# A gated mix of a long convolution and a mixer MLP: the transforms' second steps as 32x32 products

## The chip, the cores and the metric

The kernel runs on one core of one Trainium2 chip. The metric is the device time of one execution in microseconds (us); before the change the median of three runs is 244.84 us (244.6 to 245.31).

## The reference, cut to what matters

Shapes: S = 2048 tokens, D = 640 channels, F = 1536; everything is bf16.

```python
g = sigmoid((x * gate_w).sum(-1, keepdims=True))          # x is A_q
# A: a short convolution of k over 4 tokens, times v, then a long causal convolution
k_shift = sum over t of k_pad[:, t:t+S, :] * shift_k[:, 3-t]
kv = k_shift * v
y  = irfft(rfft(kv padded to 2S) * rfft(ssm_k padded to 2S))[:S] + kv * ssm_D
a  = x * y
# B: a shift mixer and an MLP
h  = gelu(layernorm(x) @ w1)
hs = concat(the four quarters of h, shifted by +1, -1, +2, -2 tokens) @ w2
x1 = x + hs
b  = x1 + gelu(layernorm(x1) @ w3) @ w4
out = g * a + (1 - g) * b
```

## The kernel before, in words

Tokens lie as 128 partitions x 16 rows ("u"), so a row of 128 tokens x 640 channels is one tile. The work is some 1,000 small tasks (`add(...)`), and `ORDER` lists for each engine, by task number, the order in which it does them. `Plan.schedule` replays these lists with prices written beside each task, and uses the result only to hand out buffers and to emit the instructions. All PSUM tiles come from one tag, `pm`, of four buffers, each of two banks: a buffer holds 128 x 640 as two halves of 320 (`HD`).

Branch B: `norm`, `first_product` (w1), `second_product` (w2), `norm` again, `third_product` (w3, called for four groups of four rows) and `fourth_product` (w4, three tasks of eight matmuls for each row). For twelve rows an addition of the row (line 941) follows on VectorE and then a scaling by 1-g (`scaled`); the last four rows (`early`: 14, 15, 0, 1) are finished by one fused instruction (line 998).

Branch A: the long convolution is a discrete transform of length 4096 in two steps. `step1` multiplies with 128 x 128 sine tables `F1` (line 803), for the filter (H) and for kv (X), and stores into the DRAM tiles `SH` and `SX`. The second step is 32 small transforms. `forward` (line 869) loads 16 frequencies with all channels (`read_b`, lines 858 to 862) and does two matmuls of 128 x 128 x 320 for each of 32 values of t, for H and for X; the stationary matrices `M2`, `G1`, `G2` are block-diagonal, 3/4 zeros, and are made from sines by copies under masks (lines 424 to 428 and 499 to 502). Each pair of filter results is copied to SBUF scaled (line 888), and two DMAs exchange its lower and upper 64 partitions into a second copy (lines 891 and 892, 32 DMAs in all). The X result is copied to SBUF, one product on VectorE (line 906) multiplies it with the filter and with its exchanged copy, and four matmuls (line 914) go back; the result is copied and stored into `SZ`. At the end `SZ` is loaded, transformed by `F1T` (line 972), scaled by the gate, multiplied with x and added.

The first `RUNS` tasks on TensorE are matmuls of the identity (line 360) that compute nothing which is used; a list can put them anywhere.

Of the kernel before, what the change touches and what calls it, by code (L numbers as in the profile page):

```python
# [10 lines left out]
ALU = mybir.AluOpType  # L11
# [8 lines left out]
        48 49 40 41 43 42 51 77 81 80 117 121 53 59 65 83 171 165 177 175 173 135 90 131 357 361 368 363 372  # L20
        370 366 359 364 185 179 149 189 145 191 187 375 381 377 193 390 388 203 386 384 205 163 272 399 397
        395 393 273 406 402 408 274 404 199 201 275 413 415 417 411 418 285 213 422 426 420 424 207 215 288
        432 436 217 434 430 219 286 801 445 61 287 439 443 446 450 807 448 816 56 454 57 452 459 813 457 804
        461 463 66 504 300 313 301 470 810 472 298 466 479 481 477 475 314 312 512 510 490 311 499 491 493
        497 299 839 845 518 842 851 848 854 619 629 624 617 622 634 639 524 526 532 534 632 627 642 637 649
        538 654 540 659 546 548 797 652 821 664 552 662 657 674 877 679 560 562 883 684 934 689 568 880 576
        886 699 692 677 704 582 709 892 707 719 712 724 588 729 697 717 596 889 722 739 744 604 602 737 610
        608 742 752 747 764 869 769 757 762 767 780 874 924 946 918 921 915 930 959 927 973 912 942 975 967
        969 982 989 984 1000 998 1007 1005 897
    """,  # L30
    "DVE": """
        96 34 47 13 37 107 39 44 108 109 110 111 52 115 114 78 45 118 119 64 122 123 58 84 72 124 125 126
        136 137 129 138 132 133 139 140 128 86 87 89 91 146 142 147 324 143 325 150 151 152 153 154 326 327
        328 156 379 329 160 330 161 157 222 331 159 225 332 228 333 231 334 335 234 336 283 277 237 279 62
        281 243 337 60 338 240 339 68 340 341 441 342 267 343 55 264 344 54 345 346 261 294 255 347 252 67
        348 349 350 258 249 296 246 468 351 352 290 506 353 354 830 292 355 835 782 484 488 825 486 495 793
        783 795 791 520 792 69 305 790 303 820 796 307 320 787 794 785 781 789 614 786 309 615 63 620 863
        625 788 630 640 784 635 858 644 650 645 873 318 660 655 798 554 868 316 647 831 665 669 670 322 667
        675 680 672 566 685 690 687 694 574 682 695 700 705 580 710 702 714 590 715 720 730 594 725 734 732
        735 727 740 749 750 826 901 745 754 759 755 760 765 896 770 772 911 864 906 952 954 902 938 955 961  # L40
        962 859 907 836 956 963 976 977 970 971 1015 991 1017 992 993 985 1001 1008 1002 1009 986 1011 1013
    """,
    "PE": """
        23 32 33 16 18 50 31 28 29 22 26 76 21 30 79 27 17 116 25 120 24 82 172 164 170 176 174 85 134 88
        130 356 367 360 20 362 369 371 365 358 188 184 178 148 190 144 186 19 374 376 378 380 192 389 387
        202 385 383 220 221 204 162 158 223 224 398 394 396 392 226 227 229 405 401 230 407 198 403 200 232
        233 414 412 235 416 410 236 212 241 242 421 425 214 419 423 206 238 239 431 435 216 433 429 218 800
        799 440 444 265 266 438 805 262 263 442 806 449 815 253 254 814 447 259 260 811 453 812 451 250 458
        251 802 456 803 460 462 256 257 503 247 248 808 244 245 469 467 809 471 465 827 828 505 478 829 480
        476 832 474 833 511 509 834 822 823 487 483 824 489 817 496 485 498 818 492 494 819 837 838 519 844  # L50
        843 840 841 517 850 849 846 847 852 853 613 618 860 861 623 628 862 616 621 633 855 638 525 523 856
        533 531 857 631 626 643 641 636 648 870 539 537 653 871 658 872 545 651 865 547 866 553 867 663 646
        661 551 876 656 668 673 875 678 666 882 559 671 561 881 683 565 879 567 688 878 686 885 693 573 575
        884 681 698 691 676 703 890 581 579 708 891 701 706 713 718 711 589 723 696 587 728 887 716 593 595
        888 733 731 721 738 726 743 898 603 748 601 899 609 736 900 607 751 741 753 893 758 763 746 894 768
        756 895 761 766 908 771 909 903 910 904 913 905 914 922 923 916 920 917 919 928 929 958 960 951 925
        953 926 939 972 943 966 974 940 941 968 981 944 990 988 945 983 999 997 1004 1006 931 932 935 933
        936 937
    """,
    "POOL": """  # L60
        15 14 46 35 36 71 73 112 113 74 127 93 94 92 95 167 141 182 155 168 166 169 180 183 195 38 194 197
        181 196 276 208 210 211 75 289 209 302 315
    """,
    "SP": """
        0 6 1 7 2 8 3 4 9 10 97 99 98 5 70 373 11 12 100 382 101 391 400 102 409 103 284 278 282 280 427 104
        437 501 515 105 428 455 106 464 297 268 271 473 295 482 291 269 293 270 500 529 502 513 514 508 507
        521 516 306 308 530 304 522 543 310 527 528 536 535 773 557 544 541 542 549 558 550 571 556 555 774
        572 317 323 563 564 586 569 570 775 578 585 577 776 583 584 321 599 591 592 777 598 319 597 600 778
        606 605 611 612 779 947 949 950 948 964 965 979 980 995 996 978 957 1018 994 1016 1003 1010 1012 987
        1014  # L70
# [109 lines left out]
def kernel(  # L180
# [22 lines left out]

    nc = tc.nc
# [35 lines left out]
    XPR = WS[0][:].rearrange("p (s a d) -> p s a d", s=4, d=D)  # L240
    HTA = WS[1][:].rearrange("p (n d) -> p n d", d=D)
    W4 = WS[1][:].rearrange("p (k d) -> p k d", d=D)
    GEN = [WS[2][:, 2048 * t:2048 * t + 2048].bitcast(I32) for t in range(3)]
# [4 lines left out]
    M2 = const("M2", [P, KH, 2, 4, 16], BF16)  # L248
    G1 = const("G1", [P, KH, 4, 2, 16], BF16)
    G2 = const("G2", [P, KH, 4, 2, 16], BF16)  # L250
# [15 lines left out]
    SH = dram.tile([32, P, D], BF16, name="SH")  # L266
    SX = dram.tile([32, P, D], BF16, name="SX")
    SZ = dram.tile([4, 32, 32, D], BF16, name="SZ")

    sizes = {"g": S, "xnt": DT * 512, "r": D, "u4": 4 * P, "xp": 0}  # L270
    counts = {"g": 3, "xnt": 2, "r": 6, "u4": 2, "xp": 4, "pm": 4}
# [53 lines left out]
    LW1 = dma("SP", 800, lambda: W1N, lambda: B_w1.rearrange("(kt p) n -> p kt n", p=P))  # L325
    QL += [load_q(2), load_q(3)]
    HNB, LH = [], []
    for dt in range(DT):
# [5 lines left out]
        tensor=B_w2.tensor, offset=B_w2[0, 0].offset, ap=[[D, P], [CG * D, 4], [1, D]])),  # L334
           dma("SP", 160, lambda: W2P[:, 4, :], lambda: bass.AP(
               tensor=B_w2.tensor, offset=B_w2[P, 0].offset, ap=[[CG * D, 4], [D, R], [1, D]]))]
# [41 lines left out]
    names = ["basep", "basei", "offp0", "offi0", "offp1", "offi1", "midp", "kli", "klf"]  # L378
    cmask = [3, 15, 4, 64, 4, 64, 120, 48, 3]
    cmul = [16.0, 512.0, -512.0, -64.0, -512.0, -64.0, 0.125, 0.0625, 1.0]  # L380
    cadd = [1.0, 1.0, 6144.0, 6144.0, 8192.0, 4096.0, 0.0, 0.0, 0.0]
# [4 lines left out]
    mk = const("mk", [P, 2, 4])  # L386
    val = {n: cv[:, i:i + 1] for i, n in enumerate(names)}

    def do_rows(e):
        for dst, vals in ((cm[:, 0, :], cmask), (ca[:, 0, :], cmul), (ca[:, 1, :], cadd)):  # L390
            i = 0
            while i < NC:
                j = i
                while j < NC and vals[j] == vals[i]:
# [5 lines left out]
    icf, ick, icn, m1 = (GEN[0][:, 0:512], GEN[0][:, 512:1024], GEN[1][:, 0:512],  # L400
                         GEN[1][:, 512:1024].bitcast(F32))

    def do_iota(e):
        nc.gpsimd.iota(icf.rearrange("p (g i n) -> p g i n", i=4, n=16), pattern=[[64, 8], [4, 4], [512, 16]],
                       base=0, channel_multiplier=0)
        nc.gpsimd.iota(ick.rearrange("p (g i n) -> p g i n", i=4, n=16), pattern=[[64, 8], [4, 4], [0, 16]],
                       base=0, channel_multiplier=0)
        nc.gpsimd.iota(icn.rearrange("p (m n) -> p m n", n=16), pattern=[[0, KH], [1, 16]],
                       base=0, channel_multiplier=0)
# [3 lines left out]
    def do_consts(e):  # L413
# [4 lines left out]
        nc.vector.scalar_tensor_tensor(out=val["basei"], in0=val["kli"], scalar=16.0, in1=val["basei"],  # L418
                                       op0=ALU.mult, op1=ALU.add)
# [4 lines left out]
    def do_masks(e):  # L424
        for n, kl in enumerate((val["klf"], val["kli"])):
            for j in range(4):
                nc.gpsimd.tensor_scalar(out=mk[:, n, j:j + 1], in0=kl, scalar1=float(j), scalar2=None,
                                        op0=ALU.is_equal)

    t_consts = add({"DVE": 1.0}, do_consts, [t_rows, t_pidx])  # L430
    t_masks = add({"POOL": 1.3}, do_masks, [t_consts])
# [17 lines left out]
    for o in range(2):  # L449
        ph[0].append(add({"ACT": 0.73, "DVE": 0.45}, lambda e, o=o: affine(  # L450
            e, GEN[0][:, 512 * o:512 * o + 512], m1, 1.0, val[f"offi{o}"]), [t_m1] + ph[2]))
    p0 = add({"DVE": 0.45}, lambda e: nc.vector.tensor_scalar(
        out=GEN[1][:, 0:512], in0=m1, scalar1=0.0, scalar2=None, op0=ALU.add), [t_m1])
    ph[1].append(add({"DVE": 0.45}, lambda e: nc.vector.tensor_scalar(
        out=GEN[1][:, 512:1024], in0=m1, scalar1=6144.0, scalar2=None, op0=ALU.add), ph[0] + [p0]))

    def step1_phase():
        g = genf()
# [434 lines left out]
    for t in range(KH):  # L893
        kg = t // 4
        if t % 4 == 0:
            zg = buf("ct")
# [139 lines left out]
```

## Time and profile before

| | |
|---|---|
| median of three runs | 244.84 us |
| the profiled execution | 245.43 us |
| its span of instructions | 243.6 us |
| granted TensorE clock in it | 0.997 |
| matmuls | 1,513, busy 230.6 us |
| VectorE (DVE) busy | 195.4 us |
| ScalarE (ACT) busy | 170.0 us |
| GpSimd (POOL) busy | 46.8 us |
| moved by DMA | 62.21 MB, mean 255 GB/s |

The span runs from the first to the last instruction of the program; 1.8 us of the profiled time lie around it. Busy time of TensorE counts each matmul up to its modelled end, so that matmuls overlap; where a step from one start to the next is given below, it is the difference of two starts, or of merged lengths. Weight loads (PEld) are listed by themselves.

### The profile page before, as it was taken

What the parts mean: (1) busy time and instruction counts of PE and PEld (TensorE: products, weight loads), DVE (VectorE), ACT (ScalarE), POOL (GpSimd) and SP (SyncE); (2) the same over time, 40 slices, a digit from 0 to 9 for tenths busy, and PEclk for the clock granted to TensorE, in tenths of its full rate; (3) what the DMA queues carried; (4) which work ended last, traced back from release to release, by engine and by line L of the source; (5) the groups of instructions that cost most, each with busy time, mean ns of one, the idle gap of its engine ahead of it and who ended that gap; (6) DMA issues with size and microseconds to landing.
All of it is one profiled execution on the core that took longest, in us unless ns stands there. A gap on an engine that the chain in (4) does not pass through costs nothing.

```text
span 243.6 us, 4200 instructions
## 1 busy us (share of the span) xinstructions
PE 230.6 (95%) x1513; PEld 144.1 (59%) x1530; DVE 195.4 (80%) x334; ACT 170.0 (70%) x256; POOL 46.8 (19%) x103
## 2 busy tenths in 40 slices
PE   7999698879999999999999999999999899999992
PEld 3666454556555556677545777655667576456771
DVE  7999999969899979997897857887887753029892
ACT  6599886879879498884554787687996740467450
POOL 8508129933271500000420000000000000000000
PEclk9999999999999999999999999999999999999998
DMA  5999869809889997689899399999999827990244
GB/s 198 401 397 280 339 163 349 275 27 309 260 222 288 341 350 263 174 302 281 278 265 275 97 235 340 264 335 269 357 261 263 271 78 243 344 377 8 108 155 172
DMA packets 38263, 62.21 MB, mean 255 GB/s; under 512 B 12739, under 2 KB 28355, under 8 KB 38242
## 3 DMA queue, kind: packets, MB, share of 16 engines
q1 hardware_dynamic: 35378, 57.84, 76.0%
q10 hardware_dynamic: 2640, 3.28, 3.8%
q0 software_dynamic: 224, 0.82, 0.9%
q8 instruction: 12, 0.20, 0.4%
q14 instruction: 9, 0.07, 0.1%
HBM read 35.71 MB, written 18.35 MB: 222 GB/s over the span
## 4 chain that ended last, share of the span: by engine, by line
PE 71%; ACT 9%; POOL 6%; DVE 5%; DMA 5%; issue 2%; SPq 0%; DVEq 0%; POOLq 0%; ACTq 0%
PE pm L697 19%; PE pm L682 18%; PE pm L660 7%; PE pm L803 5%; DMA vt<-vt 5%; PE pm L623 4%; PE pm L869 4%; PE pm L914 4%; POOL GS L643 4%; PE pm L972 4%; PE pm L360 3%; DVE W L906 2%; ACT ar L298 2%; ACT W L298 1%; PE pm L723 1%
## 5 line engine op out<-in xcount | busy, mean ns | idle before, releaser
L697 PE MATMUL pm<-W,g 128*128 128x320 bf16 x384 | 57.9, 299 | 0.0
L682 PE MATMUL pm<-xnt,W 128*128 128x512 bf16 x228 | 54.9, 379 | 0.5
L697 PEld LDWEIGHTS <-g 128*128 128x128 bf16 x384 | 37.6, 98 | 14.9
L298 ACT CAST ar<-pm 128x640 bf16<-128x640 f32 x57 | 37.1, 709 | 11.4 <-PE pm L803 9.6
L612 ACT ACTIVATE g<-pm 128x1024 bf16<-128x1024 f32 x24 | 24.5, 1026 | 20.2 <-PE pm L682 19.9
L682 PEld LDWEIGHTS <-W 128*128 128x128 bf16 x240 | 23.5, 98 | 23.7
L906 DVE TENSOR_TENSOR W<-W,vt 128x1280 bf16<-128x1280 bf16 x32 | 25.7, 820 | 6.6 <-DMA vt<-vt 4.9
L660 PE MATMUL pm<-W,GS 128*128 128x320 bf16 x160 | 24.9, 299 | 1.4 <-POOL GS L643 1.2
L767 DVE TENSOR_TENSOR ct<-kt,kt 128x640 bf16<-128x640 bf16 (+3 forms) x25 | 22.7, 944 | 0.0
L914 PE MATMUL pm<-W,G 128*128 128x320 bf16 x128 | 21.1, 299 | 0.6 <-DVE W L906 0.6
L300 ACT ACTIVATE vt<-pm 128x640 bf16<-128x640 f32 x24 | 16.5, 705 | 7.4 <-PE pm L869 6.5
L660 PEld LDWEIGHTS <-GS 128*128 128x128 bf16 x160 | 15.4, 98 | 8.9 <-POOL GS L643 1.8
L643 POOL COPY GS<-u 32x512 bf16<-32x512 bf16 (+4 forms) x20 | 16.9, 854 | 16.3 <-ACT u L612 15.7
L623 PE MATMUL pm<-xnt,W 128*128 128x512 bf16 x76 | 19.2, 379 | 0.8 <-ACT xnt L298 0.4
L803 PEld LDWEIGHTS <-F 128*128 128x128 bf16 x128 | 12.5, 98 | 11.6 <-issue 4.7
L298 ACT CAST ct<-pm 128x640 bf16<-128x640 f32 x23 | 15.4, 697 | 5.3 <-PE pm L914 5.0
L767 DVE TENSOR_TENSOR ct<-ct,ct 128x2560 bf16<-128x2560 bf16 x12 | 18.2, 1518 | 0.2
L298 ACT CAST W<-pm 128x640 bf16<-128x640 f32 x23 | 15.9, 698 | 2.5 <-PE pm L869 2.5
L665 DVE SCALAR_TENSOR_TENSOR Q<-pm,Q 128x640 bf16<-128x640 f32 x16 | 13.1, 821 | 4.4 <-PE pm L660 2.8
L869 PEld LDWEIGHTS <-M 128*128 128x128 bf16 x128 | 12.5, 98 | 6.7 <-issue 0.2
L551 DVE TENSOR_SCALAR r<-Q,mv,rs 128x640 bf16<-128x640 bf16 x32 | 15.5, 505 | 1.0 <-POOL rs L538 0.9
L914 PEld LDWEIGHTS <-G 128*128 128x128 bf16 x128 | 12.4, 98 | 6.6 <-DVE W L906 1.0
(106 smaller groups left out, 339.5 us busy)
## 6 DMA issues: line engine op xcount, KB each, us to landing
cc<-SH SPq DMA_DIRECT2D x8, 640.0 KB, 5.8
kt<-SX SPq DMA_DIRECT2D x8, 640.0 KB, 5.5
vt<-vt SPq DMA_DIRECT2D x32, 160.0 KB, 4.8
SZ<-ct SPq DMA_DIRECT2D x7, 640.0 KB, 5.8
W<-in_B_w_dram SPq DMA_DIRECT2D x2, 1920.0 KB, 12.7
SH<-ar SPq DMA_DIRECT2D x6, 640.0 KB, 4.2
SX<-ar SPq DMA_DIRECT2D x6, 640.0 KB, 3.9
g<-in_A_ssm_k_dram SPq DMA_DIRECT2D x5, 512.0 KB, 10.4
```

The costliest lines, as they stand in the source:

```text
L298: nc.scalar.copy(out=o, in_=i)
L612: nc.scalar.activation(out=o, in_=i, func=ACT.Gelu_apprx_tanh)
L623: nc.tensor.matmul(ps.tile[:, j, :], lhsT=w, rhs=xv()[:, dt, :], start=(dt == 0), stop=(dt == DT - 1))
L643: lambda o, i: nc.gpsimd.tensor_copy(out=o, in_=i)), [t, t_edges], [u4])
L660: nc.tensor.matmul(ps.tile[:, h, 0:HD], lhsT=GS[:, nt, u, :], rhs=W2P[:, nt, h * HD:(h + 1) * HD], start=(nt == 0), stop=(nt == DT - 1))
L682: nc.tensor.matmul(ps.tile[:, j, :], lhsT=W3[:, dt, (f + j) * P:(f + j + 1) * P], rhs=xv()[:, dt, :], start=(dt == 0), stop=(dt == DT - 1))
L697: nc.tensor.matmul(ps.tile[:, h, 0:HD], lhsT=gv[:, ft % 4, i * P:(i + 1) * P], rhs=W4[:, ft, h * HD:(h + 1) * HD], start=(ft == 0), stop=( ...
L767: nc.vector.tensor_tensor(out=o, in0=a, in1=b, op=op)
L803: nc.tensor.matmul(ps.tile[:, comp, 0:HD], lhsT=F1[:, comp, :], rhs=src()[:, 2 * hf + n, h * HD:(h + 1) * HD], start=True, stop=True)
L869: nc.tensor.matmul(ps.tile[:, h, 0:HD], lhsT=M2[:, t].rearrange("p a b c -> p (a b c)"), rhs=tokens(b.tile[:])[:, t % 4, h * HD:(h + 1) * ...
L906: prods = [add({"DVE": 0.75}, lambda e, t=t, xp=xp, hv=hv: nc.vector.tensor_tensor(out=XPR[:, xp.slot, 1:3, :], in0=XPR[:, xp.slot, 0:1, : ...
L914: nc.tensor.matmul(ps.tile[:, h, 0:HD], lhsT=gm[:, t].rearrange("p a b c -> p (a b c)"), rhs=XPR[:, xp.slot, 1 + a, h * HD:(h + 1) * HD], ...
```

## The change

1. **Second step.** `forward` now takes a group of 16 frequencies (kg) and one half h of the channels and does sixteen matmuls of 32 x 32 x 320, one for each pair of row quadrant kl and column quadrant i, into two `pm` buffers. The way back does thirty-two such matmuls into two buffers, two sums of sixteen. `M2`, `G1`, `G2` lose their zeros; masks and masked copies go.
2. **Exchanged filter rows.** The 32 exchanging DMAs go. A second stationary matrix `M2S`, with sine and cosine columns exchanged, gives the exchanged rows by a second `forward` for H, which is copied out of PSUM as well.
3. **Residual.** `fourth_product` begins with two matmuls of the identity with the row, so that the addition on VectorE goes; the scaling by 1-g now reads PSUM. Fused endings remain for rows 0 and 1 only; their `fourth_product` comes after the product with x, which goes into `XQ`.
4. **Layouts.** `SH`, `SX` and `SZ` are partition-major; the products' operands have eight slots, four of them in a new tile `XP2`, which also holds the phases (`GEN`); so the load of w3 no longer waits for the sines. The filter matrix for `F1T` is transposed without a copy before it.
5. **Order.** `ORDER` is new for all engines (955 tasks).

```diff
-    counts = {"g": 3, "xnt": 2, "r": 6, "u4": 2, "xp": 4, "pm": 4}
+    counts = {"g": 3, "xnt": 2, "r": 6, "u4": 2, "xp": 8, "pm": 4}
...
-    LW3 = dma("SP", 1920, lambda: W3, ..., [SIN[2], SIN[3], SIN[4]])
+    MB.append(add({"DVE": 0.6, "ACT": 1.2}, do_m2s, [MB[0]]))
+    LW3 = dma("SP", 1920, lambda: W3, ...)
...
-            prev = add({"PE": 1.09}, mm, done[f0 // 2:f0 // 2 + 2] + [w4, prev], [ps, G[f0 // 4]])
+                for h in range(2 if f0 == 0 else 0):
+                    nc.tensor.matmul(ps.tile[:, h, 0:HD], lhsT=IDB[:], rhs=qrow(u)[:, h * HD:(h + 1) * HD],
+                                     start=True, stop=False)
...
+            prev = add({"PE": 1.09 if f0 else 1.36}, mm, done + [w4, prev] + after, [ps, G[f0 // 4]])
...
-                tensor=dst.tensor, offset=dst[r0, 0, 0].offset, ap=[[D, P], [P * D, 4], [1, D]]),
+                tensor=dst.tensor, offset=dst[0, r0, 0].offset, ap=[[32 * D, P], [1, 4 * D]]),
...
-            ap=[[P * D, 32], [4 * D, 4], [1, 4 * D]]), after, [b])
+            ap=[[D, P], [P * D, 4], [1, D]]), after, [b])
...
+    def quad(i):
+        return slice(32 * i, 32 * i + 32)
+
+    def forward(kg, h, mat, b, ld, dests, after):
+        ps = [buf("pm"), buf("pm")]
         def mm(e):
-            for h in range(2):
-                nc.tensor.matmul(ps.tile[:, h, 0:HD], lhsT=M2[:, t].rearrange("p a b c -> p (a b c)"),
-                                 rhs=tokens(b.tile[:])[:, t % 4, h * HD:(h + 1) * HD], start=True, stop=True)
-        return ps, add({"PE": 0.272}, mm, [ld] + MB[0], [b, ps, dest])
+            for kl in range(4):
+                for i in range(4):
+                    nc.tensor.matmul(ps[kl // 2].tile[quad(i), kl % 2, 0:HD],
+                                     lhsT=mat[quad(kl), 4 * kg + i].rearrange("p a b -> p (a b)"),
+                                     rhs=tokens(b.tile[:])[quad(kl), i, h * HD:(h + 1) * HD],
+                                     start=True, stop=True)
+        return ps, add({"PE": 0.26}, mm, [ld, MB[0] if mat is M2 else MB[3]] + after, [b] + ps + dests)
...
-            HS[t // 2] = [dma("SP", 80, lambda a=a, hv=hv: hv()[64 * (1 - a):64 * (2 - a), 1, :, :],
-                              lambda a=a, hv=hv: hv()[64 * a:64 * (a + 1), 0, :, :], HS[t // 2], [hb]) for a in range(2)]
+            for a, mat in ((0, M2), (1, M2S)):
+                ps, last_h[kg] = forward(kg, h, mat, *BH[kg], [hb], [])
+                for q in range(2):
+                    HS[kg, h].append(add({"ACT": 0.61, "DVE": 0.75}, lambda e, a=a, q=q, ps=ps, hv=hv: copy(
+                        e, hv()[:, a, 2 * q:2 * q + 2, :], half(ps[q]), 1.0 / S), [last_h[kg]], [ps[q], hb]))
...
+                for a, gm in ((0, G1), (1, G2)):
+                    for i in range(4):
+                        for kl in range(4):
+                            k = kl % 2
+                            nc.tensor.matmul(ps[i // 2].tile[quad(kl), i % 2, 0:HD],
+                                             lhsT=gm[quad(i), 4 * kg + kl].rearrange("p a b -> p (a b)"),
+                                             rhs=XPR[xp[kl // 2].slot][quad(i), 1 + a, k * HD:(k + 1) * HD],
+                                             start=(a == 0), stop=(a == 1))
+            z = add({"PE": 0.47}, mm, prods + MB[1:3], xp + ps + [zg])
...
-    early = set(US[3])
+    early = set(US[3][2:])
...
-            if k < 3:
-                t = add({"DVE": 0.76}, lambda e, u=u, ps=ps: nc.vector.tensor_tensor(
-                    out=halves(qrow(u)), in0=half(ps), in1=halves(qrow(u)), op=ALU.add), [t4] + Y[k][3], [ps])
...
-            scaled[u] = add({"ACT": 0.7, "DVE": 0.28}, lambda e, u=u: copy(
-                e, qrow(u), qrow(u), OMG[:, u:u + 1]), [t, t_gate] + Y[k][3])
+                scaled[u] = add({"ACT": 0.65, "DVE": 0.85}, lambda e, u=u, ps=ps: copy(
+                    e, halves(qrow(u)), half(ps), OMG[:, u:u + 1]), [t4, t_gate] + Y[k][3], [ps])
```

Of the new lists, what the prediction uses, by the tasks' contents:

- SP, at the start: the second and first half of q's rows 0 to 3, filter parts 0 and 1, rows 4 to 7 of q, filter parts 2, 3, 4, q's last group, w1, q's third group. Before, w1 and the third group of q came ahead of filter parts 3 and 4.
- POOL, at the start: the small constants and three iotas now come ahead of the identity matrix.
- PE: ahead of the first matmul of `third_product`'s second group, two of the `RUNS` fewer than before, three forward rounds (before: four times two matmuls) and the residual of four rows. From there to the last matmul of the way back: 24 tasks of `third_product`, 24 of `fourth_product`, 45 forward rounds, 16 returns, 2 of the `RUNS`. After it: 12 of `third_product`, 16 last transforms, 12 of `fourth_product`. In two places rounds follow one another with nothing large between: nine tasks (seven forward, two back) and, with one of the `RUNS` in it, eight (six and two).
- Evictions and products of the second step: VectorE had 26 of the 96 evictions and now has 53 of 128; ScalarE had 70 and now has 75. The 32 products stay with VectorE.

## The prediction

> **What bounds the kernel now.** I read the page's busy shares, then the stretches between landmarks, then the timeline of TensorE.
>
> ```profile
> PE 230.6 (95%) x1513; PEld 144.1 (59%) x1530; DVE 195.4 (80%) x334; ACT 170.0 (70%) x256; POOL 46.8 (19%) x103
> ...
> PE   7999698879999999999999999999999899999992
> ```
>
> PE is nearly always busy, but matmuls overlap in that count, so what matters is the step from start to start. Two neighbours in the timeline, and the groups of transposes:
>
> ```profile
> 140.56 1.25 PE L697 MATMUL pm<-W,g 128*128 128x320 bf16 x8
> 141.65 1.25 PE L914 MATMUL pm<-W,G 128*128 128x320 bf16 x8
> ...
> L869 PE MATMUL pm<-kt,M 128*128 128x320 bf16 x64 | 13.1, 299 | 0.1
> ...
> 22.46 0.72 PE L579 MATMUL pm<-IDB,r 128*128 128x128 bf16 x10 [0.28 <-ACT u L612]
> ```
>
> Eight products of 320 columns take 141.65 - 140.56 = 1.09 us, 0.136 each, though one lasts 0.299. Five of 512 columns take 1.08. The transposes step by (0.72 - 0.22)/9 = 0.056: the quickest weight load and matmul seen here.
>
> With 1.079 for a task of `third_product`, 1.087 for one of `fourth_product`, 0.272 per pair of products, 0.543 for four and 0.432 for a warm-up, I sum TensorE's work in three stages. Stage 1 goes to the first matmul of `third_product`'s second group (117.8), stage 2 to the last on the way back (199.05), stage 3 to the end.
>
> ```profile
> 0.00:50.00 50.00, 43.01 (x310) 25.37 (x313) 46.63 (x105) 39.82 (x56) 28.90 (x83) 1.00 0.84 293
> 50.00:117.80 67.80, 67.13 (x431) 42.69 (x438) 61.09 (x90) 53.69 (x92) 13.86 (x16) 1.00 0.82 259
> 117.80:199.00 81.20, 80.24 (x516) 50.71 (x520) 64.55 (x108) 57.96 (x86) 3.99 (x5) 1.00 0.94 264
> 199.00:243.60 44.60, 40.22 (x260) 25.36 (x260) 23.16 (x33) 18.54 (x23) 0.00 (x0) 0.98 0.52 192
> ```
>
> (Columns: stretch, length, busy PE, PEld, DVE, ACT, POOL, clock, DMA share, GB/s.) Stage 1: 105.3 of work in 117.8, the hole being the start (DVE is busy 46.6 of the first 50 us). Stage 2: 80.25 in 81.2. Stage 3: 40.1 in 40.3, then 4.2 of last eviction and store. From 50 us on the array is full: there the time is TensorE's work.
>
> **The change part by part.**
>
> *Second step.* Before: 128 forward products and 128 back, 256 x 0.136 = 34.8 us. After: 1,280 pairs of a weight load and a product of 32x32x320. No row shows such a pair. Low end: sixteen at once, a round at the step of one product, 0.136, a return at 0.272: 48 x 0.136 + 16 x 0.272 = 10.9 us. High end: no overlap, 1,280 x 0.136 = 174 us; the quickest pair seen gives 1,280 x 0.056 = 71.7. I take the prices in the diff, 0.26 and 0.47 (16 ns a pair): 48 x 0.26 + 16 x 0.47 = 20.0 us. They are the planner's, not measured here; but its other prices meet their rows (0.272 for 0.272, 1.08 for 1.079, 0.57 for ten transposes, 0.545 for 0.543), and 0.26 and 0.47 are no simple share of those. This is the weakest step.
>
> *Evictions.* 96 become 128.
>
> ```profile
> L302 DVE CAST W<-pm 128x640 bf16<-128x640 f32 x9 | 7.4, 823 | 4.3 <-PE pm L869 4.2
> ...
> L298 ACT CAST W<-pm 128x640 bf16<-128x640 f32 x23 | 15.9, 698 | 2.5 <-PE pm L869 2.5
> ...
> L906 DVE TENSOR_TENSOR W<-W,vt 128x1280 bf16<-128x1280 bf16 x32 | 25.7, 820 | 6.6 <-DMA vt<-vt 4.9
> ...
> L941 DVE TENSOR_TENSOR Q<-pm,Q 128x640 bf16<-128x640 f32 x12 | 9.9, 822 | 7.0 <-PE pm L697 7.0
> ```
>
> Back to back DVE steps by 0.735, ACT by 0.59. DVE: 27 more evictions +19.8, twelve additions gone -8.9, scalings from PSUM +3.6, masks and small copies -6.0, others -5.4: about +3 over the kernel. ACT: +9 evictions, fewer masks, about +1. Neither is the bound on the whole, but in stage 2 DVE's list grows by 12 us to 63.6 at these steps, ACT's stays at 53.
>
> *Residual.* +2 products for each of 16 rows: 4.35 us on the full array. A row's first task now waits for all six GELUs of its group; the new list has it behind the group's twelve tasks anyway, so nothing.
>
> *Exchange.* 32 DMAs of 160 KB, half a microsecond of SP each, go; so does DVE's wait for them (4.9 us). DMA was 94% busy in stage 2, so this eases it; by itself it is worth nothing, as TensorE had other work queued. SH and SX exchange 1,280 byte and 5,120 byte pieces between store and load: bytes equal, taken as nothing. If loads grew by a store's spread (4.2 to 6.9 us), a load fetched a group ahead still hides it.
>
> *Start.* w1 and a part of q are issued behind filter parts 3 and 4, which wait for transposes to free their buffer (SP issued those at 9.52 before, w1 at 3.55). So `first_product` starts some 6 us later; step 1 of the filter is put in its place. The identity comes after the iotas, about 3 us later, which delays warm-ups only. Against that DVE has 4 us less to do in stage 1, and POOL loses the masks (2.4 us in the chain near 46). Stage 1's work is unchanged: two warm-ups less (-0.86), three rounds for eight products (-0.3), residual of four rows (+1.1). I take zero, from -3 to +4.
>
> *Stage 2.* 24 x 1.079 + 24 x 1.087 + 2 x 0.43 + 8 rows' residual 2.2 + 45 x 0.26 + 16 x 0.47 = 74.2. To this comes a new wait: four `pm` buffers are two rounds, and both engines together empty a round in 2/(1/0.59 + 1/0.735) = 0.655 us. Where large tasks lie between, this is hidden; in the runs of nine and eight rounds TensorE waits 8 x 0.655 - 2.76 = 2.5 and 7 x 0.655 - 2.93 = 1.65. Queued behind it on PE is a row of `fourth_product`. With the 1.0 of before: 74.2 + 4.1 + 1.0 = 79.3, a gain of 1.9 only, but five tasks of `fourth_product` more (5.4 us) lie in this stage.
>
> *Stage 3.* 12 x 1.079 + 12 x 1.087 + 16 x 0.543 + 1.1 = 35.8, and 0.3 lost as before: a gain of 4.2. The loads of SZ must hide behind twelve tasks, 12.95 us:
>
> ```profile
> 203.50 1.76 SPq L310 DMA_DIRECT2D cc<-SZ  x4
> ```
>
> Issued 4.45 us after the last return, 1.8 to issue, at most 5.8 to land: 12.05. Covered by 0.9 us; without cover each microsecond counts.
>
> *Sum.* 117.8 + 79.3 + 36.1 + 4.2 = 237.4 for a span of 243.6: -6.2. The profiled time was 245.43, 1.8 about its span, and the median 244.84; I take the difference from the median: **238.6 us**.
>
> A rule that speaks against the change: the Trainium skill, "TensorEngine Tiling (Array Packing)", Key Properties, says that changing the tiling mode drains the array. No run shown here changes it; the rival below is priced from rows.
>
> **The rivals.**
>
> *Drain between modes (slower).* Rounds alternate with large products: 91 changes in stage 2, 89 of them outside the two runs. If each waits out a product, it costs 0.299 - 0.136 = 0.163: +14.5, 253 us. It decides from 6.2/89 = 0.07 us a change. For it: steps here are all of one mode. Against: 0.26 is about twice the bare 0.136 and may hold it.
>
> *Dear pairs (slower).* At 56 ns a pair, stage 2 costs 1,232 x 0.056 = 69.0 in place of 19.2, less the 4.1 of waits: 284 us. Break-even is 16 + 6,200/896 = 23 ns (896 pairs outside the runs). Against: that step is the stream of 128 columns, not an issue limit.
>
> *No overlap: the change does not do what it says.* Pairs in one row quadrant follow one another four at a time; if a load must wait for a product in the same rows, rounds are serial at 0.136 a pair: +148, 387 us. Against: the loads here, 98 ns on all 128 rows, hide fully behind products in those rows (0.136 steps). The Trainium skill, "TensorE: Matmul & The Clock Gate", Part 3, has loads overlap only when the row group differs; by that letter it would come out so, and the trace disagrees for full loads.
>
> *VectorE's list.* If DVE keeps its idle time of stage 2 (81.2 - 64.55 = 16.65, waits for matmuls), its 12 us come on top: 93.2 for 79.3, 252.5. For it: two buffers a round, released by the later engine. Against: that idle time came from a full PE.
>
> *Cheap rounds (faster).* At 0.136 and 0.272, outside the runs 32 x 0.124 + 12 x 0.198 = 6.4 less: 232.2.
>
> **How the numbers follow.** Forecast 0.50 (0.47 faster, 0.02 same, 0.01 slower; own range 234 to 243.5), cheap rounds 0.14, drain 0.17, VectorE 0.08, dear pairs 0.07, no overlap 0.04. Faster 0.47 + 0.14 = 0.61, same 0.02, slower 0.37. A measurement of this kernel can tell about 0.3%, 0.7 us. The range goes from the cheap rounds, 232, to the drain, 253; beyond lie dear pairs, no overlap and tails.
>
> **What would show it.** Right: starts within a round some 16 ns apart, a forward round near 0.26 and a return near 0.47; PE idle about 2 us in each of the two runs of rounds; stage 2 at 79 us with DVE about 80% busy; the last transforms straight behind `third_product`. Wrong: gaps of over 0.07 at each change between large and small products (drain); steps over 23 ns inside rounds; ACT and DVE named as releasers in front of rounds throughout stage 2; the last transforms waiting for DMA; a first stage longer than 122 us.

## The result, and the profile after

The changed kernel takes 254.93 us (median of four runs, 253.12 to 255.47), the kernel before 245.07 beside it: ratio 1.038, 95% interval 1.032 to 1.045. It is slower by 10 us; the forecast was 238.6. The profiled execution took 255.47 us, its span 253.7. (One execution of experiment 4 below, 258.84 us, fell into a slower state of the chip and is left out there.) The busy shares, the second view of the page and the prediction's stretches, with the landmarks where they now lie:

```profile
PE 236.4 (93%) x2586; PEld 132.1 (52%) x2586; DVE 202.3 (80%) x330; ACT 176.0 (69%) x264; POOL 46.4 (18%) x92
...
PE   3959999899978999999999899999989999999994
...
PEclk9997999999999999999999779999995999999999
```

```profile
0.00:50.00 50.00, 41.46 (x298) 25.54 (x299) 43.97 (x102) 41.58 (x58) 24.14 (x70) 0.97 0.81 272
50.00:123.26 73.26, 70.46 (x499) 43.51 (x497) 69.74 (x113) 56.61 (x101) 22.22 (x22) 1.00 0.81 268
123.26:214.12 90.86, 88.56 (x1581) 40.79 (x1565) 69.95 (x94) 60.71 (x86) 0.00 (x0) 0.92 0.61 168
214.12:253.70 39.58, 35.94 (x244) 22.23 (x228) 18.65 (x23) 17.08 (x21) 0.00 (x0) 1.00 0.59 216
```

| length in us | before | forecast | after |
|---|---|---|---|
| stage 1 | 117.8 | 117.8 | 123.26 |
| stage 2 | 81.2 | 79.3 | 90.86 |
| stage 3 with its tail | 44.6 | 40.3 | 39.58 |

Stage 3 came out as forecast. Stage 2 is 11.6 us longer than forecast, stage 1 5.5. TensorE looks about as busy as before (93%, before 95%), yet its clock, the row `PEclk` of the page's second part, drops three times. In the first timeline rows of stage 2 single rounds stand between tasks of `third_product`:

```profile
122.97 0.35 PE L861 MATMUL pm<-cc,M2S 32*32 32x320 bf16 x16
123.26 1.25 PE L665 MATMUL pm<-xnt,W 128*128 128x512 bf16 x5
124.44 0.35 PE L861 MATMUL pm<-cc,M2S 32*32 32x320 bf16 x16
```

The sixteen pairs themselves are quick: 0.29 us from the first to the next large product. But the round starts 1.18 us after the five large ones began, whose own step is 1.079. The period is 124.44 - 122.97 = 1.47, so one round costs 1.47 - 1.079 = 0.39 us, not 0.26. No engine and no buffer is named as waited for. A return alone costs 0.53 (0.43 to the next start, and the same 0.10 ahead).

The first run of rounds:

```profile
139.44 0.49 PE L909 MATMUL pm<-XP,G 32*32 32x320 bf16 x32
140.13 0.33 PE L861 MATMUL pm<-kt,M 32*32 32x320 bf16 x8 [0.20 <-DVE vt L304]
140.62 0.33 PE L861 MATMUL pm<-kt,M 32*32 32x320 bf16 x8 [0.16 <-ACT g L595]
140.93 0.75 PE L909 MATMUL pm<-W,G 32*32 32x320 bf16 x32
141.80 0.49 PE L861 MATMUL pm<-cc,M2S 32*32 32x320 bf16 x16
142.50 0.66 PE L861 MATMUL pm<-cc,M 32*32 32x320 bf16 x16 [0.21 <-ACT ct L298]
143.11 0.78 PE L861 MATMUL pm<-kt,M 32*32 32x320 bf16 x16
143.71 0.92 PE L861 MATMUL pm<-cc,M2S 32*32 32x320 bf16 x16
144.70 0.66 PE L861 MATMUL pm<-cc,M 32*32 32x320 bf16 x16
145.45 0.64 PE L861 MATMUL pm<-kt,M 32*32 32x320 bf16 x16
146.18 0.69 PE L680 MATMUL pm<-Q,IDB 128*128 128x320 bf16 x2
146.67 2.34 PE L684 MATMUL pm<-W,g 128*128 128x320 bf16 x8
148.94 0.49 PE L861 MATMUL pm<-cc,M2S 32*32 32x320 bf16 x16
```

Nine tasks take 146.18 - 139.44 = 6.74 us, one for each 0.75 (forecast 5.26). The releasers are DVE and ACT, as expected for rounds paced by their evictions, but one of them is a GELU (line 595): in these 6.74 us VectorE is busy 6.52 and ScalarE 6.25, with a GELU and products of the second step between the evictions. What was not expected are the last two rows: from the start of the eight products to the next start it is 148.94 - 146.67 = 2.27 us, where 1.09 and 0.10 ahead of a round would be 1.19. The trace gives a granted clock of one half from 142.69 to 149.51 and again from 190.47 to 197.30, around and behind each run of rounds, and from 19.81 to 23.22 at the start: 17.1 us.

### The profile page after: what moved, and what is told of

Its sections match the earlier page's. It is cut to its first block, busy times and chain, and to the rows that moved or that the text cites. A ratio compares the mean times of both kernels' runs of the same rounds, so it can differ in the third digit from the quotient of the medians.

```text
span 253.7 us, 6250 instructions
## 1 busy us (share of the span) xinstructions
PE 236.4 (93%) x2586; PEld 132.1 (52%) x2586; DVE 202.3 (80%) x330; ACT 176.0 (69%) x264; POOL 46.4 (18%) x92
## 4 chain that ended last, share of the span: by engine, by line
PE 70%; DVE 15%; ACT 5%; issue 4%; DMA 3%; POOL 1%; ACTq 0%; POOLq 0%; DVEq 0%
PE pm L684 22%; PE pm L665 21%; DVE ct L754 9%; PE pm L643 5%; PE pm L861 5%; PE pm L965 3%; PE pm L790 3%; DMA g<-in_A_ssm_k_dram 3%; PE pm L362 3%; PE pm L680 2%; PE pm L909 2%; DVE sts L497 2%; DVE r L534 1%; PE pm L710 1%; DVE Q L648 1%
## 5 line engine op out<-in xcount | busy, mean ns | idle before, releaser
L684 PE MATMUL pm<-W,g 128*128 128x320 bf16 x384 | 61.5, 310 | 0.0
L298 ACT CAST ar<-pm 128x640 bf16<-128x640 f32 x61 | 40.3, 702 | 9.3 <-PE pm L790 7.0
L300 ACT ACTIVATE vt<-pm 128x640 bf16<-128x640 f32 x38 | 25.9, 703 | 13.0 <-PE pm L861 12.8
L304 DVE TENSOR_SCALAR vt<-pm 128x640 bf16<-128x640 f32 x26 | 21.3, 822 | 9.4 <-PE pm L861 8.3
L626 POOL COPY GS<-u 32x512 bf16<-32x512 bf16 (+4 forms) x20 | 20.1, 1020 | 14.3 <-ACT u L595 13.7
L298 ACT CAST ct<-pm 128x640 bf16<-128x640 f32 x19 | 12.8, 692 | 8.5 <-PE pm L909 7.5
L362 PE MATMUL pm<-IDB 128*128 128x512 bf16 x36 | 12.3, 478 | 4.2 <-POOL IDB L352 4.2
L304 DVE TENSOR_SCALAR ct<-pm,G 128x640 bf16<-128x640 f32 x4 | 3.5, 881 | 13.9 <-PE pm L965 13.9
L790 PE MATMUL pm<-vt,F 128*128 128x320 bf16 x64 | 12.6, 299 | 1.8 <-DVE Q L648 1.8
L506 ACT ACTIVATE W<-Q,xs 128x640 bf16<-128x640 bf16 x16 | 13.3, 830 | 1.3 <-DVE Q L648 1.1
```

What stands on the lines that cost most here:

```text
L298: nc.scalar.copy(out=o, in_=i)
L300: nc.scalar.activation(out=o, in_=i, func=ACT.Copy, scale=scale)
L304: nc.vector.tensor_scalar(out=o, in0=i, scalar1=scale, scalar2=None, op0=ALU.mult)
L362: nc.tensor.matmul(b.tile[:, 0, :], lhsT=IDB[:], rhs=IDB[:].unsqueeze(1).to_broadcast([P, 4, P]), start=True, stop=True)
L626: lambda o, i: nc.gpsimd.tensor_copy(out=o, in_=i)), [t, t_edges], [u4])
L684: nc.tensor.matmul(ps.tile[:, h, 0:HD], lhsT=gv[:, ft % 4, i * P:(i + 1) * P], rhs=W4[:, ft, h * HD:(h + 1) * HD], start=False, stop=(ft = ...
```

## The experiments

**1. Rounds by themselves.** A small kernel that computes nothing of the reference, only stretches of large products (128x128x320) and rounds: rounds back to back, one round then eight large products, two rounds then eight, rounds paced by two evictions, and two large products paced in the same way. Three of the loops:

```python
for n in range(10):              # one round, eight products: PS[0..1], PS[2]
    round_(PS[0], PS[1], n % 4)
    big(8, PS[2])
for n in range(8):               # two rounds, eight products
    round_(PS[0], PS[1], n % 4)
    round_(PS[2], PS[3], n % 4)
    big(8, PS[0])
for n in range(20):              # paced: a round, and its two evictions
    j = 2 * (n % 2)
    round_(PS[j], PS[j + 1], n % 4)
    evict(n, PS[j], PS[j + 1])
```

> Not the computation, only matmuls on its inputs and some evictions: 40 rounds of sixteen 32x32x320 products back to back without a wait; ten times one round and eight products of 128x128x320; eight times two rounds and eight products; 20 rounds paced by two evictions each; 20 pairs of 128x128x320 products paced the same way; large products between. If rounds are dear only at their borders: 0.26 to 0.29 us a round back to back, 1.087 + 0.39 = 1.48 us for one round and eight products, 1.75 for two and eight. If a pair has a price of its own (23 ns or more): 0.37 or more back to back. The clock: if the gate goes by time in which the array works, it stays at full in the dense rounds and falls in both paced sections; if it goes by how much of the array works, it stays in the paced large pairs (some 40% of the time) and falls in the paced rounds alone.

The timeline of TensorE, one round and then two:

```profile
50.39 0.35 PE L75 MATMUL pm<-X,K 32*32 32x320 bf16 x16
50.67 1.26 PE L70 MATMUL pm<-X,K 128*128 128x320 bf16 x8
51.86 0.35 PE L75 MATMUL pm<-X,K 32*32 32x320 bf16 x16
...
69.51 0.49 PE L75 MATMUL pm<-X,K 32*32 32x320 bf16 x32
69.93 1.26 PE L70 MATMUL pm<-X,K 128*128 128x320 bf16 x8
71.12 0.49 PE L75 MATMUL pm<-X,K 32*32 32x320 bf16 x32
```

The period is 1.478 with one round and 1.613 with two. Less the eight products (1.087) that is 0.391 and 0.526. So a second round adds 0.135, which is the step of one full product: the sixteen pairs do overlap fully. The remaining 0.391 - 0.135 = 0.256 is paid once for each visit, with one round in it or with two, 0.128 for each change between large and small products, with nothing else running. Of the periods expected for dear borders, 1.48 holds and 1.75 does not: the pairs themselves cost half of the 0.26 to 0.29 that it took for a round. The row of 40 rounds back to back missed its expectation in both points: its pairs start 10 ns apart, with long stops between (last section), and the clock in it is half from 32.55 to 42.79 us. The Trainium skill, "TensorEngine Tiling (Array Packing)", Key Properties, says that a change of the tiling mode drains the array: the trace agrees, with 0.128 us for each change.

**2. More borders against the same borders.** Is this price on the path of the whole kernel? One identity product for each of the 48 forward rounds, put into the middle of the round or ahead of it:

```diff
             for kl in range(4):
+                if kl == 2:     # the twin: kl == 0
+                    nc.tensor.matmul(ps[1].tile[:, 1, 0:HD], lhsT=IDB[:], rhs=tokens(b.tile[:])[:, 0, 0:HD],
+                                     start=True, stop=True)
                 for i in range(4):
```

> Kernel: the one after, with one identity product of 128x128x320 (its result is overwritten) in the middle of each of the 48 forward rounds, between its eighth and ninth 32x32 pair. So each forward round has two more changes between large and small products. It is read against its twin, which has the same product ahead of the first pair and so no further change. Theory A (a change of product size costs about 0.128 us, and TensorE's list sets the time): 48 products at 0.136 are 6.5 us, 96 changes at 0.128 are 12.3 us; outside the two runs of rounds (35 rounds, the only ones sure to be on the path) 4.8 and 9.0 us. The runs themselves keep their clock better, as the array has more to do there, which gives back up to 2.4 us. 264 to 272 us, and 9 to 12 us above the twin. Theory B (a round is long for its sixteen pairs, a change costs nothing): as the twin, 257 to 261 us, within 1 us of it.

> Kernel: the one after, with one identity product of 128x128x320 ahead of the first pair of each of the 48 forward rounds: work of 48 x 0.136 = 6.5 us more for TensorE, and, outside the runs of rounds, no further change between large and small products; inside the runs two further changes for each round. Theory A (changes cost 0.128 us): +4.8 us outside the two runs; inside them the changes and the products fill time in which TensorE waited, and keep the clock full, which gives back up to 2.4 us: 256 to 260 us. Theory B (changes cost nothing): 256 to 260 us as well; the two theories part in the difference to the twin, 9 to 12 us by A, within 1 us by B.

Measured: 271.73 us (270.93 to 274.39) in the middle, 259.73 (258.84 to 259.91) ahead: 12.0 us between two kernels with the same instructions. Counted in the traces, TensorE changes between large and small products 98 times in the kernel after, 122 times in the twin (inside the runs of rounds a product ahead of a round has two borders as well) and 194 times with the product in the middle. So 72 changes part the two, not 96, and 12.0 us are 0.167 for each, more than the 0.128 of experiment 1. One task of `third_product` with its round, the round split:

```profile
123.58 1.25 PE L665 MATMUL pm<-xnt,W 128*128 128x512 bf16 x5
124.76 0.33 PE L864 MATMUL pm<-cc,M2S 32*32 32x320 bf16 x8
125.02 0.31 PE L861 MATMUL pm<-cc,IDB 128*128 128x320 bf16 x1
125.26 0.33 PE L864 MATMUL pm<-cc,M2S 32*32 32x320 bf16 x8
125.52 1.25 PE L665 MATMUL pm<-xnt,W 128*128 128x512 bf16 x5
```

and in the twin:

```profile
122.52 1.25 PE L665 MATMUL pm<-xnt,W 128*128 128x512 bf16 x5
123.60 0.30 PE L861 MATMUL pm<-cc,IDB 128*128 128x320 bf16 x1
123.83 0.35 PE L864 MATMUL pm<-cc,M2S 32*32 32x320 bf16 x16
124.12 1.25 PE L665 MATMUL pm<-xnt,W 128*128 128x512 bf16 x5
```

The periods are 125.52 - 123.58 = 1.94 and 124.12 - 122.52 = 1.60, so two further changes cost 0.34 us, and the 35 rounds outside the runs make 35 x 0.34 = 11.9 of the 12.0 us. Two borders of 0.128 are 0.26 of the 0.34; whether the other 0.08 is a half round that takes more than half of a whole one is not separated. The twin is 4.8 us above the kernel after, which is the work of its 35 products outside the runs, 35 x 0.136. So changes do cost time, and TensorE's list sets the time where rounds stand alone.

**3. Keeping the clock.** Two identity products ahead of each of the 17 tasks in the two runs of rounds, into the PSUM that the round then overwrites: more work for TensorE, where it waits anyway.

```diff
+    def fill(ps, rows):
+        for n in range(2):
+            nc.tensor.matmul(ps[n].tile[:, 0, 0:HD], lhsT=IDB[:], rhs=rows[:, n, 0:HD], start=True, stop=True)
...
         def mm(e):
+            if what in FILL_F:      # the 13 forward rounds in the runs; four returns likewise
+                fill(ps, tokens(b.tile[:]))
```

> The kernel after, with two more products of 128x128x320 (identity, result overwritten) ahead of each of the 17 rounds in the two runs of rounds that follow one another: 34 x 0.136 = 4.6 us of array work that is of no use. Theory A (the clock is halved for 6.8 us twice because the array works too little while these runs wait for evictions): the clock stays at 1.00 from 25 us on; the work put in fills waits; 250 to 252.5 us against 254.9. Rival B (the rounds cost what they cost, the clock falls whatever lies between them): the clock falls at 142 and 190 us as before, and the extra products come on top: 255 to 260 us.

Measured: 252.5 us (250.8 to 254.4), ratio 1.028 (1.020 to 1.036), at the upper end of Theory A's range. In its profile the clock is full from 22.95 us on, and the eight products behind the first run take their usual time:

```profile
147.36 0.35 PE L872 MATMUL pm<-kt,M 32*32 32x320 bf16 x16
147.80 0.43 PE L680 MATMUL pm<-Q,IDB 128*128 128x320 bf16 x2
148.07 1.25 PE L684 MATMUL pm<-W,g 128*128 128x320 bf16 x8
149.25 0.35 PE L872 MATMUL pm<-cc,M2S 32*32 32x320 bf16 x16
```

Adding 34 products made the kernel 2.4 us faster, though the runs of rounds with their fillings now take 7.58 us (140.22 to 147.80) in place of 6.74 and 6.98 (186.00 to 192.98) in place of 6.09. Two of its four executions had full clock from start to end and took 250.8 and 251.0, the others 254.0 and 254.4. So the start was filled as well, with 13 identity products where TensorE waited for the last filter part:

```diff
+            if dt == 4:
+                for _ in range(13):
+                    nc.tensor.matmul(ps.tile[:, 0, :], lhsT=IDB[:], rhs=IDB[:].unsqueeze(1).to_broadcast([P, 4, P]),
+                                     start=True, stop=True)
             for n2 in range(N2):
```

> Kernel: the one that keeps the clock in the two runs of rounds, and in addition 13 identity products of 512 columns (13 x 0.213 = 2.8 us) ahead of the transposes of the last filter part, where TensorE waited 2.99 us for its load (from 16.2 to 19.15 us); their result is overwritten by the transposes. Theory A (half clock is part of what the longer first stage costs): the clock is full from about 5 us to the end in every execution, and the time is that of the two executions at full clock among the four of the kernel without this, 250.8 and 251.0 us: 250 to 251.5. Theory B (the first stage's loss is waits alone): the clock at 20 us is kept but the next waits take its place, as with the filter buffers: 252 to 254 us.

Measured: 253.22 us (252.39 to 253.68), the clock 0.993 to 1.000. Theory B's range holds the number: stage 1 ends at 122.28, 1.0 earlier than after, and waits of 0.80 us for the load and 0.84 for VectorE (line 721) take the place of the old one, while the stalls at 70 to 80 us stay (1.80 us at 71.23). With the clock kept everywhere the kernel is 1.7 us faster, with it kept in stage 2 alone 2.4, which the spread of the executions does not tell apart: keeping the clock in this way is worth some 2 us of the ten, net of what the fillings cost. What made two executions of the first 250.8 and 251.0 stays open.

**4. The residual back to VectorE** for rows 2 to 15, with the lists otherwise as they are:

```diff
-                scaled[u] = add({"ACT": 0.65, "DVE": 0.85}, lambda e, u=u, ps=ps: copy(
-                    e, halves(qrow(u)), half(ps), OMG[:, u:u + 1]), [t4, t_gate] + Y[k][3], [ps])
+                t = add({"DVE": 0.76}, lambda e, u=u, ps=ps: nc.vector.tensor_tensor(
+                    out=halves(qrow(u)), in0=half(ps), in1=halves(qrow(u)), op=ALU.add), [t4] + Y[k][3], [ps])
+                scaled[u] = add({"ACT": 0.7, "DVE": 0.28}, lambda e, u=u: copy(
+                    e, qrow(u), qrow(u), OMG[:, u:u + 1]), [t, t_gate] + Y[k][3])
```

> The kernel after with the residual added by VectorE again for rows 2 to 15 (rows 0 and 1 keep it on TensorE), at the place of their scaling; the rest of the order unchanged. Theory A (TensorE's array is the bound where these rows lie, the residual is 0.28 us a row on it): 14 x 0.28 = 3.9 us less work on the array, 251 to 252.5 us. Rival B (VectorE's list is as tight: 14 additions of 0.735 less 8 cheaper scalings are 7 us more for it): 256 to 260 us.

Measured: median 256.64 us (254.15 to 257.55), ratio 1.045 (1.038 to 1.052). TensorE has 3.8 us less to do, and the kernel is not faster; its median is 1.7 us longer, with ranges that overlap. Its trace shows TensorE waiting for the additions (line 938), 0.83 us at 123.95 and 0.54 at 159.91, which the kernel after does not have: with these lists more work for VectorE comes out as waits. So by itself the residual on TensorE was no loss.

**5. Buffers for filter parts 3 and 4,** so that their loads wait for no transpose:

```diff
-        b = buf("g")
+        b = buf("g" if dt < 3 else "vt")
```

> The kernel after, with filter parts 3 and 4 in two buffers of another tag (vt), so that their loads need not wait for the transposes of parts 0 and 1. Theory A (the start was lost by the new order of loads): TensorE's wait of 3.0 us at 16 us goes, and with it the half clock from 19.8 to 23.2; the first product of the third product's second group starts at 118.5 to 120 in place of 123.3; 251 to 252 us. Rival B (VectorE's list sets the first stage): the wait goes but the stage still ends at 122 to 123.5, and the time moves by less than 1 us.

Measured: 253.45 us (252.22 to 253.67), ratio 1.033 (1.030 to 1.036). The wait of the transposes for the load is gone, 3.0 us,

```profile
19.15 1.53 PE L710 MATMUL pm<-IDB,g 128*128 128x128 bf16 x16 [2.99 <-DMA g<-in_A_ssm_k_dram]
```

(this is its row in the kernel after), but stage 1 ends only 1.7 us earlier, at 121.58, between the two theories' ranges: other waits took its place, the longest new one 1.40 us at 21.27 for VectorE's addition into the filter matrix (line 717), and the half clock did not go, it moved to 21.37 to 24.78.

**6. Short gate sums.** VectorE has 113.7 us of work in stage 1 after, 107.7 before. The reason is in one line: the 16 sums of the gate ran from 110.5 to 140.1 us before, and from 103.4 to 119.3 after, since the scaling by 1-g now empties PSUM and needs its factor with the first rows. Is this what makes stage 1 longer?

```diff
-            nc.vector.scalar_tensor_tensor(out=scr.tile[:], in0=XQ[:, u, :], scalar=1.0, in1=GWB[:],
+            nc.vector.scalar_tensor_tensor(out=scr.tile[:, 0:40], in0=XQ[:, u, 0:40], scalar=1.0, in1=GWB[:, 0:40],
```

> Kernel: the one after, with the 16 sums of the gate (line 805, 0.82 us each) over the first 40 channels only, so that each becomes short; the order of all lists stays. What is left out: 600 of the 640 channels in the gate's sum. Before, 14 of the 16 sums came after the end of the first stage (110.5 to 140.1 us, two ahead of 117.8); after, all come ahead of it (103.4 to 119.3), since the scaling by 1-g now empties PSUM and so must have its factor when the first rows of the fourth product are done. Theory A (the first stage is longer because VectorE's list in it grew: 113.7 us busy against 107.7, and 95% busy from 50 us to the stage's end): some 12 us less for VectorE there, of which TensorE can win what it had lost after 50 us, 3 to 5 us: the first stage ends at 118 to 120.5 (123.26 after), total 249.5 to 252. Theory B (the first stage is longer because of the new order of loads and the filter at the start): the first stage ends at 122.5 to 124, total 254 to 255.5.

> Kernel: the one before, with the same short gate sums, as the control of the run with short sums in the kernel after. Theory A and B alike: only two of the 16 sums stood in the first stage, the others where VectorE waits for TensorE: 0 to 1 us gained, 243.8 to 245.1 us. Were it 3 us or more, the gain of short sums would say nothing of where they stand.

Measured: 254.15 us (253.53 to 254.75) for after, 245.54 for before, which is before's time. Theory A fell. VectorE's busy time from 50 us to the end of stage 1 went from 69.74 to 59.37, and that end moved only from 123.26 to 122.61. TensorE has no gap over 0.3 us between 95 us and that end in the kernel after or in this one, so whatever VectorE does there is hidden. So the loss lies elsewhere, and the stops of TensorE lie earlier. In the kernel after it stands at these places:

```profile
71.81 0.43 PE L790 MATMUL pm<-vt,F 128*128 128x320 bf16 x2 [1.80 <-DVE Q L648]
...
82.08 2.10 PE L665 MATMUL pm<-xnt,W 128*128 128x512 bf16 x9 [0.68 <-ACT W L506]
```

Ahead of the first, VectorE's list has products of the short convolution (line 754) from 60.63 to 70.93 without a break, and only then the eviction of `second_product` (line 648) for which the buffer waits. That is order, not amount.

**7. Order.** Two kernels that do the same work: filter buffers as in 5 and residual as in 4, one with the lists of the kernel after, the other with lists made anew for prices of 0.39 and 0.53. New lists also choose the engine of each eviction anew (some 40 tasks went from VectorE to ScalarE and as many the other way) and hand out the buffers anew.

> Kernel: the one after with two parts undone at once and its lists else as they are: filter parts 3 and 4 have buffers of their own, and the residual of rows 2 to 15 goes back to VectorE (14 additions, 28 identity products less). Theory A (the lists keep the runs of rounds, their half clock and the gate sums ahead of the first stage's end, so that two repairs of parts bring little): 252 to 256 us. Theory B (these parts themselves are what made the kernel slow): 248 us or less.

> Kernel: as the one with two parts undone, but with lists made anew for all engines: a round stands alone between two large tasks (no run of rounds without large products longer than two), the sixteen gate sums stand in the second stage, VectorE takes 57 evictions and ScalarE 151. The planner's prices of a round and a return, which only hand out buffers, are the measured 0.39 and 0.53 us in place of 0.26 and 0.47, and its DMA latency is 2.9 in place of 2.6. TensorE's list holds, by the measured steps, 4.35 x 14/16 = 3.8 us less than the kernel after, and 61 visits of rounds at 0.256 for their borders stay in it. Theory A (borders cost 0.256 a visit; clock, runs and stalls come from the order): no half clock between 30 us and the end, the gain over the kernel after 8 to 11 us: 244 to 247 us, as before within 1%. Theory B (the second step as 32x32 products costs more than borders and order explain): above 249 us.

Measured: 254.53 us (253.84 to 254.59) with the old lists, 244.36 us (242.56 to 246.13) with the new; before beside them 244.97, ratio for the new lists 0.998 (0.9945 to 1.001). The stages of the two, old lists first:

```profile
50.00:121.61 71.61, 67.89 (x477) 41.99 (x479) 68.63 (x113) 54.30 (x98) 20.40 (x22) 1.00 0.83 268
121.61:213.18 91.57, 86.79 (x1540) 39.56 (x1549) 73.67 (x103) 61.36 (x87) 0.00 (x0) 0.94 0.59 166
213.18:252.80 39.62, 35.53 (x224) 21.77 (x224) 20.38 (x26) 17.04 (x21) 0.00 (x0) 1.00 0.59 216
```

```profile
50.00:118.31 68.31, 65.75 (x469) 39.82 (x471) 60.32 (x78) 52.02 (x93) 21.75 (x25) 1.00 0.82 244
118.31:204.51 86.20, 82.07 (x1536) 38.21 (x1546) 76.48 (x116) 59.77 (x86) 0.00 (x0) 1.00 0.69 199
204.51:242.40 37.89, 34.64 (x221) 21.48 (x221) 24.99 (x42) 21.55 (x28) 0.00 (x0) 0.99 0.62 231
```

Stage 1 gains 3.3 us, stage 2 5.4, stage 3 1.7. The clock of stage 2 is 1.00 instead of 0.94: no more than three rounds stand together, most stand alone behind a large task, pay their 0.256, and have their evictions hidden behind that task (six of the `RUNS` lie in this stage, two in the kernel after, and they too give TensorE work beside rounds). The gate sums, which with the addition on VectorE need not come early, are spread from 131.3 to 208.3 us, and VectorE is 89% busy there. Which of these steps brings how much is not separated.

**8. Order once more,** the same work with lists made again for the same prices.

> Kernel: the same instructions as the one with new lists, with lists made once more for the same prices (0.39 and 0.53 us; VectorE takes 49 evictions of this step, ScalarE 159). Theory A (the rest of the loss is order): the replay with these prices ends 0.8 us earlier than that of the first new lists, so 0 to 2 us less than 244.4: 242.4 to 244.4 us, 0.2 to 1.0% under the kernel before. Theory B (the first new lists were at the floor of this form: 218.6 us of TensorE's work, the start, some 10 us, and the tail, 4 us, make 233 us and the rest are waits that no order removes): 244 to 246 us, no different from before.

Measured: 243.69 us (242.15 to 245.27), ratio to before 0.9935 (0.9904 to 0.9967). So the form with 32x32 rounds, its residual on VectorE and its lists made for measured prices is 0.65% faster than the kernel before, and 4% faster than the change as it was. Its twelve executions differ by the clock that they were granted: four at 1.000 took 242.15 to 242.22 us, five at 0.993 took 243.10 to 244.11, three at 0.986 took 245.19 to 245.27. The profiled one, at 0.986, has two stretches of half clock of 3.41 us each before its tail; by the mean clock the others have one or none, so some 1.5 us goes with each such stretch.

## Why the prediction was wrong

- **The price of a round.** This step failed, and it was named the weakest. It took 0.26 and 0.47 from the diff and put nothing beside them for the neighbours; measured between large products are 0.39 and 0.53, of which 0.256 is borders (experiment 1). For the 32 rounds and 12 returns that stand alone in stage 2 that is 32 x 0.13 + 12 x 0.06 = 4.9 us. The prediction had named gaps of over 0.07 at each change as a sign of being wrong. The fit of the planner's other prices to their rows was no evidence: those rows were all of one mode, this one was not.
- **The rival "drain between modes"** had the cost in the right place, at each change, and its size too high: it priced a visit at 0.26 + 2 x 0.163 = 0.59, measured is 0.135 + 2 x 0.128 = 0.39. That its 253 us comes near 254.9 is in part chance, as more than half of the loss is not borders.
- **The wait in the runs of rounds** was placed right and sized 2.5 and 1.65 us. The runs took 6.74 and 6.09 us for 5.26 and 4.58 forecast, +3.0, and the half clock behind them another 1.5 and 2.3 or so in large products. Two things were left out. 0.655 a round has both engines do nothing but evict, perfectly shared; in the first run a GELU and products of the second step stood between, and in experiment 1, where each engine had its one eviction a round, a round came each 0.73 us, VectorE's step of 0.735. And the step took the clock to stay full where TensorE waits; it did not, and in the trace of before, where the clock is half only from 242.06 us on, after TensorE's last product, nothing showed that it would.
- **The start and stage 1: "I take zero, from -3 to +4".** Measured +5.5. The late filter load was seen and is worth 1.7 us at most (experiment 5), the half clock at 20 us about 1 (experiment 3). "VectorE has 4 us less to do" was wrong by 10 us (6 more instead), because the sums of the gate were not counted when the scaling moved, but that cost 0.7 us (experiment 6). The rest, some 2 us, is put down to order: stalls such as those of 1.8 and 0.7 us at 71.81 and 82.08. That is argued from the trace; no run takes these stalls out alone, and the new lists, which bring stage 1 back to 118.3, change much at once.
- **VectorE's list** as a rival: not the bound on the whole, but experiment 4 shows that with these lists more work for it comes out as waits of TensorE.
- **Right:** TensorE's list sets the time where rounds stand alone (experiment 2); the sixteen pairs overlap, four of them in each row quadrant, so "dear pairs" and "no overlap" fell (0.135 for a second round); the evictions pace the runs; stage 3 at 36.0 us and its tail.

Together: 4.9 borders, 3.0 and 3.8 in and behind the runs of rounds make the 11.6 us of stage 2 within 0.1; with 5.5 in stage 1 and -0.7 in stage 3 they are, within 0.1, the difference of the span to the forecast, 253.7 - 237.4 = 16.3.

## What to carry to other kernels

A small matmul that is cheap in a row of its like has a second price, that of the border to its neighbours: count visits, not products. Before lists are written by a price, measure that price between the neighbours it will have. Here the same work with lists made anew took 10 us less (experiment 7); that the first lists were bad for their wrong prices is likely but not shown, as no lists were made anew for the old ones. And a step that moves into the emptying of PSUM takes its inputs with it: look for what must now be ready earlier.

## What the runs showed of the hardware that was not expected

- **A change between 128x128 and 32x32 products costs about 0.13 us** of TensorE: 0.128 for each end of a visit in experiment 1, and the 0.39 of a single round in the kernel after fits it. Where a round is split, two changes cost 0.34 (experiment 2).
- **The clock falls without a long stop.** In experiment 1, rounds paced by evictions, one for 0.73 us, and two large products in the same pace (0.272 of 0.73 us, 37% of the time) both fell to half clock, mean 0.61 and 0.68:

```profile
86.77:104.23 17.46, 12.85 (x334) 5.06 (x334) 14.71 (x20) 13.37 (x20) 0.00 (x0) 0.61 0.01 3
115.60:131.54 15.94, 13.55 (x50) 5.63 (x48) 14.71 (x20) 13.31 (x20) 0.00 (x0) 0.68 0.04 15
```

  So it is not the small mode, but how little the array does; whether its share of the time counts or the short stops between is not separated. The Trainium skill, "TensorE: Matmul & The Clock Gate", Part 1, has the clock halve after an idle window; here the array never stood for more than 0.65 us in these two stretches, and the clock fell all the same, with large products at 37% use. The half-clock stretches in the kernel after, 3.41 and 6.83 us, are one and two of the windows that the Trainium skill gives in the same part (3.4 us).
- **Long rows of small products stop and go.** Back to back the pairs of experiment 1 start 10 ns apart at full clock, but after each 128 or so TensorE stands 0.6 to 2.45 us, and the profile shows nothing that it waits for ("issue"): 128 pairs take 3.7 to 4.0 us, 29 to 31 ns each. The cause is open. Sixteen or thirty-two at a time between large products do not show this.
